# Query and den projection of batches 1 to 3 in one group of sixteen 32x32 TensorE tiles, and a new order of all steps

## The chip, the cores and the metric

The kernel runs on one core of one Trainium2 chip. The metric is the device time of one execution in microseconds, as the median of several runs. A core has five engines with a queue each: PE (TensorE, matrix products into PSUM), DVE (VectorE), ACT (ScalarE), POOL (GpSimd) and SP (SyncE, which here issues most DMAs). Each queue is worked off in order, and an instruction waits until what it reads is written and what it overwrites has been read.

## The reference

Two layers follow each other: a polynomial-sketch attention with 4 batches, 4 heads, 1088 tokens and head size 32 (r = 8), and a feed-forward layer of width 2048 with the activation h * sigmoid(beta * h).

```python
def phi(x):
    a = np.einsum('rd,bhsd->bhsr', S1, x)
    b = np.einsum('rd,bhsd->bhsr', S2, x)
    return np.einsum('bhsi,bhsj->bhsij', a, b).reshape(*x.shape[:-1], r * r)
q_p, k_p = (phi(q), phi(k))
kv = np.einsum('bhsf,bhsd->bhfd', k_p, v)
z = np.sum(k_p, axis=2)
num = np.einsum('bhsf,bhfd->bhsd', q_p, kv)
den = np.einsum('bhsf,bhf->bhs', q_p, z)[..., None] + 1e-06
x = (num / den).transpose(0, 2, 1, 3).reshape(4352, 128)
...
h = x @ w_in
g = h * (1.0 / (1.0 + np.exp(-beta * h)))
return (g @ w_out).astype(np.float32)
```

There is no softmax: kv and z of a batch are sums over all its tokens, so the queries of a batch can only be finished after its keys.

## The kernel before, in words

Attention runs in float32, the feed-forward layer in float16. Tokens of a batch sit on 128 partitions, 34 each; a transpose on DVE turns q and k so that head and feature lie on the partitions (turn_q, turn_k: tokens tq, tk). All work is cut into named steps, and one string, SEQ, is the order in which the steps are written out; each engine gets its instructions in that order, so the string fixes the order of every queue. In the string a token such as `qp2` is the step for batch 2. Where a step can run on two engines, lower case is the first one (POOL for products, ACT for copies) and upper case the second (DVE).

The steps of a later batch b (1 to 3) are these.

- kp, ka (kps, kab): the keys times S1 and S2 on PE, turned on DVE into KAB.
- o (outer): the products of both halves of KAB, 64 features for each key, in four parts, on POOL or DVE.
- va, vb, vc, np, nz: kv on PE (kvz, L586), copied, turned by PE (ndps) and copied into ND.
- g, gm, wz, wm: z is not summed from the 64 features. PE forms the 8x8 products of the two halves over all tokens (gram_g, L599), DVE masks them (gmz), and PE multiplies by S2 (wz_g, L705). This gives W', with which den of a query is the sum over i of (S1 q)_i times (W' q)_i. wm masks W' into a 128x32 matrix with gm.
- qp, qa (qps L488, qab L517): the queries times S1 and S2 in 8 matmuls of 64 rows and 32 columns, turned on DVE into QAB.
- c, ct (c_g L726, c_t L736): the queries times W' in 4 matmuls of 128 rows and 32 columns, turned on DVE.
- cm, cr, cd (L740 to L749): the product with S1 q, the sum, 1e-6 and the reciprocal, and S1 q scaled with it. So the division is done before the features are formed.
- p, t (outer, turn_qo): the 64 features of the queries in four parts, and their transposes on DVE into QT.
- n (num_g, L769): the product with ND in 2 x 16 matmuls of 32x32, into four PSUM banks. x (put_x) copies this into xT, the input of the second layer.

Batch 0 goes another way (aa, ba, ca, ma, da, ia, ra, na, xa and the same with b), and in the first 16 us beta is prepared, w_in is scaled by it (u0 to u3, POOL) and w_out by its inverse (w0 to w7; ACT, or DVE in upper case). `~` is one matmul on constants that keeps PE busy.

The second layer is spread between these steps. A `+` (first, w1) is a "wave": two matmuls of 128x512 into one of two PSUM buffers of two banks, and a Silu on ACT over both (L424, L433). A `-` (second, w2) is two matmuls that add the oldest waiting wave to the output of its chunk of 512 tokens (moeout, L400). There are 68 waves; a `+` does nothing while the tokens of its chunk are not ready. A wave is named here by chunk and number: 6.0 is the first of chunk 6. What is left of both when the string ends follows in a loop (rest).

PSUM has eight banks: four for the two wave buffers (which nps, aps, bps share), two for the buffer "two", one for "one", one for moeout. A buffer is handed on when the last reader of its old content is done, wherever that reader stands in the string.

Of the kernel before, what the change touches and what calls it, by code (L numbers as in the profile page):

```python
# [9 lines left out]
F32 = mybir.dt.float32  # L10
F16 = mybir.dt.float16
ACTF = mybir.ActivationFunctionType
MUL = mybir.AluOpType.mult
# [5 lines left out]
def kernel(  # L19
# [66 lines left out]
    def sb(shape, dtype, name):  # L86
        return const.tile(shape, dtype, tag=name, name=name)
# [125 lines left out]
    nc.vector.memset(hm, 0.0)  # L213
    for h in range(H):
        nc.vector.memset(hm[32 * h : 32 * h + 32, h % 2, :], 1.0)
    gm = sb([P, 4], F32, "gm")
    nc.vector.memset(gm, 0.0)
    for c in range(4):
        nc.vector.memset(gm[32 * c : 32 * c + 32, c : c + 1], 1.0)
    e3 = sb([P, 3], F32, "e3")  # L220
    nc.vector.memset(e3, 0.0)
    nc.vector.memset(e3[:, 1:2], 1.0)
# [34 lines left out]
    sk = sb([P, 2, 2, R], F32, "sk")  # L257
    skc = sk.rearrange("p n m r -> p (n m r)")
    sab = []

    def prep_s(n):
        st_ = sb([P, 4, R], F32, f"st{n}")
        nc.vector.transpose(out=st_.rearrange("p u r -> p (u r)"), in_=sr[n])
        nc.gpsimd.tensor_tensor(out=sk[:, n], in0=st_[:, :2, :], in1=hm, op=MUL)  # L264
        t = sb([P, R, R], F32, f"s{n}")
        nc.scalar.copy(out=t, in_=cut(st_, ([[1, R], [0, R]], [[0, R], [1, R]])[n]))
        sab.append(t.rearrange("p i j -> p (i j)"))

    beta_bc = sb([P, DFF], F32, "beta_bc")

# [227 lines left out]
        kT = kT2[b % 2]  # L498
        project(t, lambda rows, g: kT[rows, NJK * g : NJK * g + NJK, :])

    def qps(b, new=two):
        t = PS["qps", b] = new("qps")
        project(t, lambda rows, g: qT2[b % 2][rows, QB[g] : QB[g] + NJK, :])


    def left_copy(j0, j1, eng):
# [17 lines left out]
        KAB[b] = turn_ab(PS["kps", b], "kab")  # L524

    def qab(b):
        QAB[b] = turn_ab(PS["qps", b], "qab")


    def outer(dst, b, src, nm, j0, j1, eng=None):  # L530
        if b not in dst:
            dst[b] = sbA.tile([P, NJK, H, F], F32, tag=nm, name=nm, bufs=1)
        a0 = src[b][:, 0, j0:j1]
        n = H * (j1 - j0)
        left = cut(a0, [[R, n], [1, R], [0, R]])
        if b == 0 and eng is nc.vector:
            left = cut(KPS[0], [[R, n], [1, R], [0, R]], R * H * j0)
        (eng or nc.vector).tensor_tensor(  # L538
            out=cut(dst[b][:, j0:j1], [[F, n], [R, R], [1, R]]),
            in0=left,  # L540
            in1=cut(a0, [[R, n], [0, R], [1, R]], NJK * H * R),
            op=MUL,
        )

# [156 lines left out]
        )  # L701

    def wz_g(b):
        for g in range(4):
            nc.tensor.matmul(  # L705
                out=PS["gp", b][32 * g : 32 * g + 32, 64 : 64 + H * R],
                lhsT=sr[1],
                rhs=PS["gm", b].rearrange("p h i -> p (h i)"),
                start=True,
                stop=True,  # L710
                skip_group_check=True,
            )

    def wz_m(b):
        t = PS["wz", b] = sbA.tile([P, H, R], F32, tag="wz", name="wz")
        nc.vector.tensor_tensor(
            out=t,
            in0=cut(PS["gp", b], [[R, H], [1, R]], 64),
            in1=cut(gm, [[1, H], [0, R]]),
            op=MUL,  # L720
        )

    def c_g(b, own):
        t = PS["cps", b] = one("cps") if own else PS["kps", b][:, 0]
        for g in range(4):
            nc.tensor.matmul(  # L726
                out=t[32 * g : 32 * g + 32, :JW],
                lhsT=PS["wz", b].rearrange("p h i -> p (h i)"),
                rhs=qT2[b % 2][:, QB[g] : QB[g] + NJK, :],
                start=True,  # L730
                stop=True,
            )

    def c_t(b):
        t = PS["ct", b] = sbA.tile([P, NJK, H, R], F32, tag="ct", name="ct")
        nc.vector.transpose(out=t.rearrange("p j h i -> p (j h i)"), in_=PS["cps", b][:, :JW])  # L736

    def c_a(b, eng):
        t = PS["ct", b]
        eng.tensor_tensor(out=t, in0=t, in1=QAB[b][:, 0], op=MUL)  # L740

    def c_r(b):
        rc = PS["rc", b] = sbA.tile([P, NJK, H], F32, tag="rc", name="rc")
# [3 lines left out]

    def c_d(b, eng):
        eng.tensor_tensor(  # L749
            out=QAB[b][:, 0],  # L750
            in0=QAB[b][:, 0],
            in1=cut(PS["rc", b], [[H, NJK], [1, H], [0, R]]),
            op=MUL,
        )
# [6 lines left out]
        ND[b] = sbA.tile([P, 2, P], F32, tag="nd", name="nd")  # L761
        eng(out=ND[b], in_=t[:, : 2 * P].rearrange("p (c w) -> p c w", c=2))

    def num_g(b, tiles):
        for fc in range(2):
            for h in range(H):
                for g in (2, 0, 3, 1):
                    rows = slice(32 * g, 32 * g + 32)
                    nc.tensor.matmul(  # L769
                        out=tiles[g // 2][32 * h : 32 * h + 32, g % 2, :JW],  # L770
                        lhsT=ND[b][rows, fc, 32 * h : 32 * h + 32],
                        rhs=QT[b][rows, :, h, fc, :],
                        start=(fc == 0),
                        stop=(fc == 1),
                        skip_group_check=True,
                    )

    def put_x(b, i, t, eng):
        x0 = xT[:, b * S + 32 * QB[2 * i] :]
# [86 lines left out]
    def nd_pe(b):  # L866
        PS["ndps", b] = one("ndps")
        nd_g(b, PS["ndps", b])

    def n_g(b):  # L870
        PS["nps", b] = [two("nps"), wave2("nps")]
        num_g(b, PS["nps", b])

    ACT, DVE, POOL = nc.scalar, nc.vector, nc.gpsimd
    DO = {"+": first, "-": second, "~": lambda: keep_warm(1)}
# [24 lines left out]
    for nm, fn in (  # L900
        ("aa", a_A),
        ("ba", b_A),
        ("rb", prep_rbeta),
        ("zt", gram_terms),
        ("zz", gram_z),
        ("da", d_A),
        ("ia", i_A),
        ("kd", kd0),
        ("nd", nd0),
        ("nc", nc0),  # L910
        ("na", n_A),
        ("ab", a_B),
        ("bb", b_B),
        ("db", d_B),
        ("ib", i_B),
        ("nb", n_B),
    ):
        do(nm, fn)
# [20 lines left out]
    for b in range(1, B):  # L939
        for nm, fn in (  # L940
            ("tk", turn_k),
            ("ka", kab),
            ("tq", turn_q),
            ("qa", qab),
            ("gm", gram_m),
            ("wz", wz_g),
            ("wm", wz_m),
            ("ct", c_t),
            ("cr", c_r),
            ("va", kv_a),  # L950
            ("vb", kv_b),
            ("np", nd_pe),
            ("n", n_g),
            ("lv", load_v),
            ("lk", lambda b: load_rows(k, k_t, b, "k")),
            ("lq", lambda b: load_rows(q, q_t, b, "q")),
        ):
            do(f"{nm}{b}", fn, b)
        do2(f"kp{b}", kps, (b,), two, wave2)
        do2(f"g{b}", gram_g, (b,), True, False)  # L960
        do2(f"c{b}", c_g, (b,), True, False)
        do2(f"qp{b}", qps, (b,), two, wave2)
        do2(f"cm{b}", c_a, (b,), POOL, DVE)
        do2(f"cd{b}", c_d, (b,), POOL, DVE)
        do2(f"vc{b}", kv_c, (b,), ACT.copy, DVE.tensor_copy)
        do2(f"nz{b}", lambda b, e: put_ndg(b, PS["ndps", b], e), (b,), ACT.copy, DVE.tensor_copy)
        for n, (j0, j1) in enumerate(JR):
            do2(f"o{b}{n}", lambda b, j0, j1, e: outer(KP, b, KAB, "kp", j0, j1, e), (b, j0, j1), POOL, DVE)
            do2(f"p{b}{n}", lambda b, j0, j1, e: outer(QO, b, QAB, "qo", j0, j1, e), (b, j0, j1), POOL, DVE)
            do(f"t{b}{n}", turn_qo, b, j0, j1)  # L970
        for i in range(2):
            do2(
                f"x{b}{i}",
                lambda b, i, e: put_x(b, i, PS["nps", b][i], e),
                (b, i),
                ACT.copy,
                DVE.tensor_copy,
            )

    SEQ = """  # L980
        ~ s0 ~ bt0 tk00 s1 tk01 kp0 ka0 ~ tqa la ~ ~ lv00 lv01 ~ ~ lv02 bl0 gr ~ lv03 bt1 aa lb zt ba
        ca1 O01 o02 o00 lw1 BL1 zz ~ ca0 be0 bc0 rb v00 o04 v01 lqb ma0 o03 v02 be1 lo0 ma1 lw0 v03 tqb
        bc1 v04 lk1 lw2 da be2 ~ kd bc2 ia nd W0 u0 nc ra0 ~ be3 bc3 ra1 na xa0 xa1 ab u1 CB1 w2 cb0 +
        lq1 ~ u2 w3 lo1 tk1 lv1 bb - u3 mb1 w1 mb0 + kp1 + + ka1 g1 o13 o10 - + - tq1 w4 lv2 gm1 wz1 QP1
        nb O12 wm1 qa1 db w7 o11 + ib + c1 ct1 - lq2 w5 xb cm1 lk2 - + cr1 va1 vb1 CD1 w6 p12 lq3 + - +
        lk3 VC1 - - + np1 + p10 NZ1 - - + p11 p13 - + t12 - - t11 t10 t13 + n1 x10 x11 - + tq2 tk2 kp2 +
        - + lv3 ka2 tk3 g2 o22 + gm2 o20 qp2 wz2 o23 wm2 qa2 + - + c2 + ct2 CM2 - + kp3 + - cr2 + CD2
        p22 p21 p23 O21 - t22 + va2 vb2 vc2 + p20 ka3 + tq3 t23 - - + - t20 np2 + t21 - NZ2 - + n2 x20
        g3 gm3 + X21 wz3 wm3 qp3 + + c3 - + - + qa3 ct3 - O33 o31 + cm3 O32 - cr3 - CD3 + p32 - + O30 -
        + p30 va3 + t32 - P33 + vb3 + - VC3 P31 + - + - np3 + t31 t30 - t33 - + NZ3 n3 - X30 X31 + - - +  # L990
        + - - + - + - - + - + - + - - + - + - + - - + - + - + - - + - + - + - - + - + - + - + - - - -
    """
    for s_ in SEQ.split():
        DO[s_]()
# [30 lines left out]
```

## Time and profile before

| | |
|---|---|
| median of 3 runs | 102.26 us (101.84 to 102.65) |
| profiled execution | 102.28 us, span 100.3 us from first to last instruction |
| granted TensorE clock | 0.996 |
| busy: PE, ACT, DVE, POOL | 93.8, 79.3, 59.7, 34.7 us |
| first wave starts | 16.39 us |
| last n (nps of batch 3) ends | 73.5 us |
| PE ends | 96.77 us |
| Silu on ACT | 68 of 1.02 us, 65.6 us |

In the views, L and a number is a line of the kernel, "out<-in" are the tiles written and read, a bracket at the end is the time in which the engine sat idle before the instruction and what ended it. A float32 matmul shows as two instructions, so "x16" of kps are eight matmuls. Durations of neighbours on one engine overlap slightly.

### The profile page before, as it was taken

Reading aid. Unit: us, or ns where it says so; the run is one execution under the profiler, and the core shown is the slowest. Engines: PE = TensorE matmul, PEld = TensorE weight load, DVE = VectorE, ACT = ScalarE, POOL = GpSimd, SP = SyncE. Lnnn points to the kernel's source line nnn. Section 1 sums busy time; section 2 is a strip of 40 time slices with the busy share of each in tenths; the row PEclk is TensorE's granted clock in tenths of the full one; section 3 lists DMA queues with packets and bytes.
Section 4 is the critical chain, followed back from the end, with each engine's and each line's share of the span. In section 5 each row is a group of like instructions: output and inputs, shape, how many; then the busy total and the mean of one; then the engine's idle time right before and its main releaser. Section 6 shows DMA issues by size and latency. Waiting matters only on the chain.

```text
span 100.3 us, 2886 instructions
## 1 busy us (share of the span) xinstructions
PE 93.8 (93%) x1189; PEld 45.7 (46%) x1189; DVE 59.7 (59%) x129; ACT 79.3 (79%) x103; POOL 34.7 (35%) x41
## 2 busy tenths in 40 slices
PE   5969988999999999999999999999998999999960
PEld 2325732334365443434654434555434444545750
DVE  4759798897876985687894579559463011020220
ACT  1524758997999979899998699999847999999930
POOL 5228686569339601924990032800000000000000
PEclk9999999999999999999999999999999999999998
DMA  2999999999960780023000230006000413202243
GB/s 66 290 213 286 399 405 372 208 205 286 396 241 2 112 218 6 7 41 64 7 0 2 49 60 0 0 0 108 3 0 13 72 20 64 48 9 50 50 78 78
DMA packets 22876, 11.35 MB, mean 113 GB/s; under 512 B 18320, under 2 KB 20688, under 8 KB 22864
## 3 DMA queue, kind: packets, MB, share of 16 engines
q1 hardware_dynamic: 22480, 11.06, 42.3%
q8 instruction: 9, 0.15, 0.7%
q10 hardware_dynamic: 352, 0.11, 0.4%
q0 software_dynamic: 32, 0.02, 0.1%
q14 instruction: 3, 0.02, 0.1%
HBM read 8.95 MB, written 2.23 MB: 111 GB/s over the span
## 4 chain that ended last, share of the span: by engine, by line
PE 85%; DMA 4%; ACT 3%; DVE 2%; issue 2%; POOL 0%; DVEq 0%; POOLq 0%
PE wave L424 31%; PE moeout L400 27%; PE kvz L586 5%; PE nps L769 5%; DMA sr<-in_S_dram 4%; PE kps L488 3%; PE kvz L196 2%; PE qps L488 2%; PE cps L726 2%; PE moeout L368 2%; PE aps L562 1%; PE betaps L286 1%; PE dps L641 1%; ACT g L433 1%; PE ndps L635 1%
## 5 line engine op out<-in xcount | busy, mean ns | idle before, releaser
L433 ACT ACTIVATE g<-wave 128x1024 f16<-128x1024 f32 x68 | 65.6, 1024 | 7.1 <-PE wave L424 6.6
L424 PE MATMUL wave<-xT,winp 128*128 128x512 f16 (+1 forms) x144 | 40.1, 370 | 0.5 <-DVE xT L785 0.3
L400 PE MATMUL moeout<-g,woutp 128*128 128x512 f16 x128 | 35.7, 380 | 0.2 <-ACT g L433 0.2
L424 PEld LDWEIGHTS <-winp 128*128 128x128 f16 x144 | 15.1, 115 | 16.2 <-issue 3.9
L400 PEld LDWEIGHTS <-woutp 128*128 128x128 f16 x128 | 12.1, 98 | 14.9 <-issue 2.5
L410 DVE STREAM_TRANSPOSE o_sb<-moeout 128x512 f32<-128x512 f32 x8 | 5.7, 716 | 20.1 <-PE moeout L400 14.7
L538 POOL TENSOR_TENSOR kp<-kab 128x512 f32<-128x512 f32 (+2 forms) x11 | 12.4, 1157 | 8.7 <-DVE kab L517 6.7
L538 POOL TENSOR_TENSOR qo<-qab 128x512 f32<-128x512 f32 (+1 forms) x10 | 12.0, 1230 | 7.1 <-DVE qab L749 7.1
L549 DVE STREAM_TRANSPOSE qt<-qo 128x512 f32<-128x512 f32 (+1 forms) x12 | 8.7, 756 | 2.1 <-POOL qo L538 1.9
L196 PE MATMUL kvz<-idle 128*128 128x448 f16 x22 | 6.8, 432 | 1.1 <-DVE idle L99 1.1
L306 POOL TENSOR_TENSOR winp<-w_in_sb,beta_bc 128x512 f16<-128x512 f32 x4 | 5.2, 1317 | 2.1 <-DMA w_in_sb<-in_moe_w_in_dram 2.1
L586 PE MATMUL kvz<-kp,v 128*32 128x64 f32 x288 | 5.3, 221 | 0.0
L740 POOL TENSOR_TENSOR ct<-ct,qab 128x288 f32<-128x288 f32 x2 | 2.2, 1110 | 8.8 <-DVE ct L736 8.8
L466 DVE STREAM_TRANSPOSE qT<-q 128x1088 f32<-128x1088 f32 (+2 forms) x5 | 5.2, 1050 | 0.0
L460 DVE STREAM_TRANSPOSE kT<-k 128x1088 f32<-128x1088 f32 (+2 forms) x5 | 5.2, 1049 | 0.0
L586 PEld LDWEIGHTS kvz<-kp,v 128*32 128x32 f32 x288 | 4.3, 110 | 1.8 <-issue 1.2
L517 DVE STREAM_TRANSPOSE kab<-kps 128x288 f32<-128x288 f32 x8 | 3.3, 457 | 2.5 <-PE kps L488 2.5
L769 PE MATMUL nps<-qt,nd 32*32 32x288 f32 x192 | 4.8, 413 | 0.0
L320 ACT ACTIVATE woutp<-w_out_sb,rbeta 128x128 f16<-128x128 f32 x14 | 4.6, 398 | 0.0
L538 DVE TENSOR_TENSOR kp<-kab 128x512 f32<-128x512 f32 (+1 forms) x5 | 4.5, 922 | 0.0
L196 PEld LDWEIGHTS <-idle 128*128 128x128 f16 x22 | 2.4, 117 | 4.0 <-issue 2.2
L488 PE MATMUL kps<-kT,sk 64*32 64x288 f32 x64 | 3.1, 415 | 1.0 <-POOL sk L264 1.0
(100 smaller groups left out, 73.9 us busy)
## 6 DMA issues: line engine op xcount, KB each, us to landing
v<-in_v_dram SPq DMA_DIRECT2D x15, 144.0 KB, 5.3
k<-in_k_dram SPq DMA_DIRECT2D x3, 544.0 KB, 7.1
q<-in_q_dram SPq DMA_DIRECT2D x3, 544.0 KB, 6.4
out_dram<-o_sb SPq DMA_DIRECT2D x20, 64.0 KB, 1.9
w_out_sb<-in_moe_w_out_dram SPq DMA_DIRECT2D x2, 512.0 KB, 8.2
w_in_sb<-in_moe_w_in_dram SPq DMA_DIRECT2D x2, 256.0 KB, 4.7
w_in_sb<-in_moe_w_in_dram SPq DMA_DIRECT2D x1, 512.0 KB, 7.7
k<-in_k_dram SPq DMA_DIRECT2D x1, 288.0 KB, 2.9
```

The costliest lines, as they stand in the source:

```text
L196: nc.tensor.matmul(out=kvz0[:, F:], lhsT=idle, rhs=cut(idle, [[0, 7], [1, F]]), start=fresh, stop=True, skip_group_check=True,)
L306: eng.tensor_tensor(out=winp[:, c], in0=w_in_sb[:, c], in1=beta_bc[:, c], op=MUL)
L400: nc.tensor.matmul(out=moe["acc"][:, :tw], lhsT=woutp[:, j, :], rhs=g[jj], start=(j == 0), stop=(j == NJ - 1),)
L410: nc.vector.transpose(out=o_sb[:, :nt, :].rearrange("p t d -> p (t d)"), in_=moe["acc"][:, :tw])
L424: nc.tensor.matmul(out=wv[:, jj // per, o : o + tw], lhsT=win_unit(j0 + jj), rhs=xT[:, t0 : t0 + tw], start=True, stop=True,)
L433: nc.scalar.activation(out=g[:, :, :gw], in_=wv[:, :, :gw], func=ACTF.Silu)
L460: nc.vector.transpose(out=kT2[b % 2][:, t0:t1].rearrange("p t s -> p (t s)"), in_=k_t[b][:, t0:t1].rearrange("p t d -> p (t d)"),)
L488: nc.tensor.matmul(out=t[32 * g : 32 * g + 32, pi, :JW], lhsT=skc[rows, :], rhs=moving(rows, g), start=True, stop=True,)
L538: (eng or nc.vector).tensor_tensor(out=cut(dst[b][:, j0:j1], [[F, n], [R, R], [1, R]]), in0=left, in1=cut(a0, [[R, n], [0, R], [1, R]], NJ ...
L549: nc.vector.transpose(out=QT[b][:, j0:j1].rearrange("p j h c s -> p (j h c s)"), in_=QO[b][:, j0:j1].rearrange("p j h f -> p (j h f)"),)
L586: nc.tensor.matmul(out=KVZ[b][32 * h : 32 * h + 32, :F], lhsT=v_t[b][:, h, j, :], rhs=KP[b][:, j, h, :], start=(j == 0), stop=(j == NJK - ...
L769: nc.tensor.matmul(out=tiles[g // 2][32 * h : 32 * h + 32, g % 2, :JW], lhsT=ND[b][rows, fc, 32 * h : 32 * h + 32], rhs=QT[b][rows, :, h, ...
```

## The change

For batches 1 to 3 the query projection and the den projection become one. A 32x32 weight matrix sq per parity of the batch holds eight columns of S1, eight of S2 and eight of W', and eight of zeros. It is repeated on the four row groups, one for each head; W' differs from head to head. qps is then 16 matmuls of 32x32: the row group is the head, the column group the quarter of the tokens, and each head has a PSUM bank of its own. They fill "two" and a wave buffer. qab turns both with two transposes of 128x576. c_g, c_t, the mask gm and the masked W' go; wz_g writes eight columns per head, and wm copies them into sq. The constant columns of sq are filled once on POOL (token sq). c_a, c_d and the outer products of the queries read QAB with a step of 32. n is cut into m (first half of the features) and n. SEQ is a new string.

```diff
+    sq = [sb([P, 32], F32, f"sq{n}") for n in range(2)]
...
+    def prep_sq():
+        for t in sq:
+            nc.gpsimd.memset(t[:, 3 * R :], 0.0)
+            for n in range(2):
+                nc.gpsimd.tensor_copy(out=t[:, R * n : R * n + R], in_=st[n][:, 0, :])
...
-    def qps(b, new=two):
-        t = PS["qps", b] = new("qps")
-        project(t, lambda rows, g: qT2[b % 2][rows, QB[g] : QB[g] + NJK, :])
+    def qps(b):
+        PS["qps", b] = [two("qps"), wave2("qps")]
+        for g in range(4):
+            for h in (2, 0, 3, 1):
+                rows = slice(32 * h, 32 * h + 32)
+                nc.tensor.matmul(
+                    out=PS["qps", b][h // 2][32 * g : 32 * g + 32, h % 2, :JW],
+                    lhsT=sq[b % 2][rows, :],
+                    rhs=qT2[b % 2][rows, QB[g] : QB[g] + NJK, :],
...
     def qab(b):
-        QAB[b] = turn_ab(PS["qps", b], "qab")
+        o = QAB[b] = sbA.tile([P, NJK, H, 32], F32, tag="qab", name="qab")
+        for n in (1, 0):
+            nc.vector.transpose(
+                out=cut(o, [[32, 2], [32 * H, NJK], [1, 32]], 64 * n),
+                in_=PS["qps", b][n][:, :, :JW].rearrange("p m (j c) -> p m j c", j=NJK),
+            )
...
     def wz_g(b):
-        for g in range(4):
+        for h in range(H):
             nc.tensor.matmul(
-                out=PS["gp", b][32 * g : 32 * g + 32, 64 : 64 + H * R],
+                out=PS["gp", b][32 * h : 32 * h + 32, 64 : 64 + R],
                 lhsT=sr[1],
-                rhs=PS["gm", b].rearrange("p h i -> p (h i)"),
+                rhs=PS["gm", b][:, h, :],
...
     def wz_m(b):
-        t = PS["wz", b] = sbA.tile([P, H, R], F32, tag="wz", name="wz")
...
+        nc.vector.tensor_copy(out=sq[b % 2][:, 2 * R : 3 * R], in_=PS["gp", b][:, 64 : 64 + R])
...
-    def c_g(b, own):
...
-    def c_t(b):
...
+    def m_g(b):
+        PS["nps", b] = [two("nps"), wave2("nps")]
+        num_g(b, PS["nps", b], 0)
+
     def n_g(b):
-        PS["nps", b] = [two("nps"), wave2("nps")]
-        num_g(b, PS["nps", b])
+        num_g(b, PS["nps", b], 1)
...
+        ~ tk00 lb lv00 ~ s0 s1 lv01 bt0 tk01 ~ kp0 ~ lv02 bl0 ka0 lv03 ~ bt1 tqa ~ ~ ~ gr lqb zt ~ la
+        o02 lw0 aa BL1 ba lk1 ca0 zz be0 bc0 lw2 o00 ~ ~ CA1 v00 o04 ma0 o01 ma1 be1 tqb da ia bc1 v01
+        v02 be2 ra1 o03 bc2 v03 v04 kd u0 tk1 ra0 be3 nd nc ~ lw1 bc3 lo0 ~ na xa0 xa1 ab cb0 u2 lq1 +
+        lo1 u1 CB1 bb rb mb1 w3 + kp1 w0 mb0 + ka1 + g1 W1 nb gm1 u3 wz1 + db w2 o12 - wm1 + tq1 o11
+        w5 ib xb lv1 - lk2 lk3 O10 lq2 - sq o13 W4 - qp1 w7 + qa1 CM1 va1 vb1 w6 cr1 CD1 + - + - - P11
+        p10 - vc1 + + np1 t11 - lq3 NZ1 - + - t10 p13 p12 t13 t12 + - tk2 - + m1 n1 x10 - x11 + kp2 tq2
+        + - + ka2 g2 tk3 + o21 gm2 wz2 wm2 lv2 lv3 - + o22 qp2 qa2 - CM2 o20 cr2 + + CD2 va2 P20 o23 vb2
+        + VC2 - + - t20 + - np2 + p21 p23 - + t21 - t23 + kp3 ka3 NZ2 + p22 t22 - + - + g3 m2 gm3 n2 wz3
+        tq3 - x20 + - wm3 X21 qp3 qa3 + - + o32 - + - CM3 + O30 O33 o31 va3 cr3 + CD3 - + - + P33 - +
+        vb3 + - t33 VC3 + p32 np3 - + P31 p30 t31 t30 t32 NZ3 - + - - + m3 n3 x30 + - X31 - - + + - - +
...
```

The old string, from which the steps above are moved, begins like this and ends each batch in the order named in the prediction.

```
~ s0 ~ bt0 tk00 s1 tk01 kp0 ka0 ~ tqa la ~ ~ lv00 lv01 ~ ~ lv02 bl0 gr ~ lv03 bt1 aa lb zt ba
ca1 O01 o02 o00 lw1 BL1 zz ~ ca0 be0 bc0 rb v00 o04 v01 lqb ma0 o03 v02 be1 lo0 ma1 lw0 v03 tqb
bc1 v04 lk1 lw2 da be2 ~ kd bc2 ia nd W0 u0 nc ra0 ~ be3 bc3 ra1 na xa0 xa1 ab u1 CB1 w2 cb0 +
lq1 ~ u2 w3 lo1 tk1 lv1 bb - u3 mb1 w1 mb0 + kp1 + + ka1 g1 o13 o10 - + - tq1 w4 lv2 gm1 wz1 QP1
nb O12 wm1 qa1 db w7 o11 + ib + c1 ct1 - lq2 w5 xb cm1 lk2 - + cr1 va1 vb1 CD1 w6 p12 lq3 + - +
...
t20 np2 + t21 - NZ2 - + n2 x20
g3 gm3 + X21 wz3 wm3 qp3 + + c3 - + - + qa3 ct3 - O33 o31 + cm3 O32 - cr3 - CD3 + p32 - + O30 -
+ p30 va3 + t32 - P33 + vb3 + - VC3 P31 + - + - np3 + t31 t30 - t33 - + NZ3 n3 - X30 X31 + - - +
...
```

More of the change, by code (lines that the diff above doesn't have):

```diff
@@ L215 @@
         nc.vector.memset(hm[32 * h : 32 * h + 32, h % 2, :], 1.0)
[L216 to L219, printed above, removed]
     e3 = sb([P, 3], F32, "e3")
@@ L259 @@
     sab = []
+    sq = [sb([P, 32], F32, f"sq{n}") for n in range(2)]
+    st = []
     def prep_s(n):
@@ L267, in prep_s @@
         sab.append(t.rearrange("p i j -> p (i j)"))
+        st.append(st_)
+    def prep_sq():
[3 more added lines that the diff above has]
+                nc.gpsimd.tensor_copy(out=t[:, R * n : R * n + R], in_=st[n][:, 0, :])
     beta_bc = sb([P, DFF], F32, "beta_bc")
@@ L499, in kps @@
         project(t, lambda rows, g: kT[rows, NJK * g : NJK * g + NJK, :])
-    def qps(b, new=two):
-        t = PS["qps", b] = new("qps")
-        project(t, lambda rows, g: qT2[b % 2][rows, QB[g] : QB[g] + NJK, :])
+    def qps(b):
[7 more added lines that the diff above has]
+                    rhs=qT2[b % 2][rows, QB[g] : QB[g] + NJK, :],
+                    start=True,
+                    stop=True,
+                )
     def left_copy(j0, j1, eng):
@@ L526, in qab @@
     def qab(b):
-        QAB[b] = turn_ab(PS["qps", b], "qab")
+        o = QAB[b] = sbA.tile([P, NJK, H, 32], F32, tag="qab", name="qab")
[3 more added lines that the diff above has]
+                in_=PS["qps", b][n][:, :, :JW].rearrange("p m (j c) -> p m j c", j=NJK),
+            )
     def outer(dst, b, src, nm, j0, j1, eng=None):
@@ L541, in outer, with outer_q @@
             in1=cut(a0, [[R, n], [0, R], [1, R]], NJK * H * R),
+            op=MUL,
+        )
+    def outer_q(b, j0, j1, eng):
+        if b not in QO:
+            QO[b] = sbA.tile([P, NJK, H, F], F32, tag="qo", name="qo", bufs=1)
+        a0 = QAB[b][:, j0:j1]
+        n = H * (j1 - j0)
+        eng.tensor_tensor(
+            out=cut(QO[b][:, j0:j1], [[F, n], [R, R], [1, R]]),
+            in0=cut(a0, [[32, n], [1, R], [0, R]]),
+            in1=cut(a0, [[32, n], [0, R], [1, R]], R),
             op=MUL,
@@ L714, in wz_m, with c_a @@
     def wz_m(b):
-        t = PS["wz", b] = sbA.tile([P, H, R], F32, tag="wz", name="wz")
[L716 to L720, printed above, removed]
-        )
-    def c_g(b, own):
[L724 to L732, printed above, removed]
-    def c_t(b):
[L735 to L740, printed above, removed]
+        nc.vector.tensor_copy(out=sq[b % 2][:, 2 * R : 3 * R], in_=PS["gp", b][:, 64 : 64 + R])
+    def c_a(b, eng):
+        t = PS["ct", b] = sbA.tile([P, NJK, H, R], F32, tag="ct", name="ct")
+        eng.tensor_tensor(
+            out=t, in0=QAB[b][:, :, :, 2 * R : 3 * R], in1=QAB[b][:, :, :, :R], op=MUL
+        )
     def c_r(b):
@@ L749, in c_d @@
         eng.tensor_tensor(
-            out=QAB[b][:, 0],
-            in0=QAB[b][:, 0],
+            out=QAB[b][:, :, :, :R],
+            in0=QAB[b][:, :, :, :R],
             in1=cut(PS["rc", b], [[H, NJK], [1, H], [0, R]]),
@@ L762, in put_ndg, with num_g @@
         eng(out=ND[b], in_=t[:, : 2 * P].rearrange("p (c w) -> p c w", c=2))
[L764 to L776, printed above, removed]
+    def num_g(b, tiles, fc):
+        for h in range(H):
+            for g in (2, 0, 3, 1):
+                rows = slice(32 * g, 32 * g + 32)
+                nc.tensor.matmul(
+                    out=tiles[g // 2][32 * h : 32 * h + 32, g % 2, :JW],
+                    lhsT=ND[b][rows, fc, 32 * h : 32 * h + 32],
+                    rhs=QT[b][rows, :, h, fc, :],
+                    start=(fc == 0),
+                    stop=(fc == 1),
+                    skip_group_check=True,
+                )
     def put_x(b, i, t, eng):
@@ L903 @@
         ("rb", prep_rbeta),
+        ("sq", prep_sq),
         ("zt", gram_terms),
@@ L943 @@
             ("tq", turn_q),
+            ("qp", qps),
             ("qa", qab),
@@ L947 @@
             ("wm", wz_m),
-            ("ct", c_t),
             ("cr", c_r),
@@ L952 @@
             ("np", nd_pe),
+            ("m", m_g),
             ("n", n_g),
@@ L960 @@
         do2(f"g{b}", gram_g, (b,), True, False)
-        do2(f"c{b}", c_g, (b,), True, False)
-        do2(f"qp{b}", qps, (b,), two, wave2)
         do2(f"cm{b}", c_a, (b,), POOL, DVE)
@@ L968 @@
             do2(f"o{b}{n}", lambda b, j0, j1, e: outer(KP, b, KAB, "kp", j0, j1, e), (b, j0, j1), POOL, DVE)
-            do2(f"p{b}{n}", lambda b, j0, j1, e: outer(QO, b, QAB, "qo", j0, j1, e), (b, j0, j1), POOL, DVE)
+            do2(f"p{b}{n}", lambda b, j0, j1, e: outer_q(b, j0, j1, e), (b, j0, j1), POOL, DVE)
             do(f"t{b}{n}", turn_qo, b, j0, j1)
@@ L980 @@
     SEQ = """
[L981 to L991, printed above, removed]
+        ~ tk00 lb lv00 ~ s0 s1 lv01 bt0 tk01 ~ kp0 ~ lv02 bl0 ka0 lv03 ~ bt1 tqa ~ ~ ~ gr lqb zt ~ la
+        o02 lw0 aa BL1 ba lk1 ca0 zz be0 bc0 lw2 o00 ~ ~ CA1 v00 o04 ma0 o01 ma1 be1 tqb da ia bc1 v01
+        v02 be2 ra1 o03 bc2 v03 v04 kd u0 tk1 ra0 be3 nd nc ~ lw1 bc3 lo0 ~ na xa0 xa1 ab cb0 u2 lq1 +
+        lo1 u1 CB1 bb rb mb1 w3 + kp1 w0 mb0 + ka1 + g1 W1 nb gm1 u3 wz1 + db w2 o12 - wm1 + tq1 o11 +
+        w5 ib xb lv1 - lk2 lk3 O10 lq2 - sq o13 W4 - qp1 w7 + qa1 CM1 va1 vb1 w6 cr1 CD1 + - + - - P11
[4 more added lines that the diff above has]
+        vb3 + - t33 VC3 + p32 np3 - + P31 p30 t31 t30 t32 NZ3 - + - - + m3 n3 x30 + - X31 - - + + - - +
+        - + - + - - + - + - + - + - - + - + - + - + - - + - + - + - + - - + - + - + - + - + - - -
     """
```

## The prediction

> **What bounds the kernel now.** I read the page's busy line first, then the 40 slices, then the chain that ended last, then that chain in order of time, and last the timelines of the places that the change touches.
>
> The page says that PE is busy 93% of the span. The stretches say where: I asked for the busy time of each engine in seven windows, in the columns window, us, PE (count), PEld, DVE, ACT, POOL, granted clock, DMA share, GB/s.
>
> ```profile
> 0.00:16.40 16.40, 13.70 (x233) 6.74 (x234) 11.82 (x43) 7.46 (x19) 9.02 (x20) 1.00 0.92 286
> 16.40:24.40 8.00, 7.76 (x115) 3.01 (x115) 7.21 (x12) 7.79 (x14) 6.00 (x5) 1.00 1.02 243
> 24.40:37.00 12.60, 12.60 (x191) 6.30 (x188) 10.45 (x19) 10.90 (x14) 6.22 (x7) 1.00 0.65 202
> 37.00:55.50 18.50, 18.50 (x286) 8.49 (x289) 12.93 (x25) 17.00 (x19) 9.59 (x8) 1.00 0.12 22
> ...
> 73.50:97.00 23.50, 23.21 (x136) 12.51 (x136) 4.84 (x9) 19.99 (x21) 0.00 (x0) 1.00 0.23 39
> ```
>
> From 24.4 us on PE never pauses, at a granted clock of 1.00. ACT is second (17.0 of 18.5 us), and in 16.4 to 24.4 DVE and ACT are nearly as full as PE. So from the first wave (16.39 us) to PE's end (96.77) the time is PE's work plus its waits, and a saving on PE counts in full unless something else then comes late.
>
> The chain in order of time gives the price of each PE group, as start, length, what.
>
> ```profile
> 40.91 0.65 PE qps L488 x16
> ...
> 42.74 0.43 PE wave L424 x2
> 43.17 0.62 PE cps L726 x8
> 43.79 0.55 PE wave L424 x2
> ...
> 53.93 1.53 PE nps L769 x63
> ```
>
> A wave or a moeout pair costs 0.43 us, and 0.11 more when it follows a small-tile group (0.55). The present query projection is 0.65, the den projection 0.62. The only 32x32 group with 288 columns is nps: 32 matmuls in 64 passes in 1.53 us, 24 ns a pass.
>
> **The change, part by part.**
>
> *PE work.* (1) c_g goes: 3 x 0.62 = -1.86. (2) qps changes from 8 matmuls of 64x32 (16 passes, 0.65) to 16 of 32x32 (32 passes). By the nps row that is 32 x 24 ns = 0.77; bounds 0.65 (it costs what qps costs now) and 0.95 (0.62 of c_g added for half again as much). I take 0.77, the row of the same shape: 3 x 0.12 = +0.36. (3) wz_g keeps four matmuls, 8 columns wide instead of 32: kept at 0.20 (gp L705). (4) n splits into m and n, standing side by side: 2 x 0.77 for 1.53, nothing. (5) I counted, in the two orders, the waves and moeouts that follow a small-tile group: 19 before, 18 after: -0.11. (6) One of the keep-warm matmuls (0.29) stood after the first wave and does not any more: -0.29. The sum of (1) to (6) is -1.90. The same ledger over the old order gives 78.9 us from first wave to end against 80.38 in the trace, so 1.5 us of PE's time there is waits.
>
> The Trainium skill, "TensorE: Matmul & The Clock Gate", part 3 (Measured speedup vs the span model), says that tiles on different row and column groups run together and that each further tile adds about 4 ns. By that the new group would be about 0.65 + 8 x 0.004 = 0.68, and the whole another 0.3 us shorter; the nps row, at 24 ns a pass, speaks for a floor on the issue instead, and I stay with the row.
>
> *DVE.* qab was two transposes of 128x288 (0.46 each) and ct one (0.47). They become two of 128x576. The nearest row is the 128x576 transpose of rb, 0.78, whose successor started after 0.70; so 1.4 for the pair instead of 1.4 for the three: nothing. Bounds 1.3 (the 0.66 pitch of the 128x512 rows) and 2.0, if scattered 32-element rows are written slower. The five memsets of gm (0.06 each) go in a time when DVE waits for S anyway (0.26 us idle before L263): nothing. Moves between engines: O01 to POOL (-0.68 on DVE), one asb and two ct products to DVE (+0.75, +0.9), x30 to ACT (-0.76). They count where a chain passes, below.
>
> *POOL.* prep_sq is six small operations, 0.10 (a memset) to 0.22 (sk L264) each: 0.6 to 1.3 us, between o11 and o13, at about 22.4 to 23.6. The matmuls that need it come at about 25.4, so it is covered by 1.8 us. All five outers of batch 0 are now on POOL: 7.90 + 4 x 1.08 + 0.53 = 12.75 instead of 11.66.
>
> *The start.* v03 now needs the last outer (12.75). On PE, da, v01, v02, be2 fill the time to 13.2, then v03 and v04 end at 13.6. The copy kd stands behind bc2 on ACT (13.27 to 13.86), so it runs at about 13.85 instead of 13.61; nd, two keep-warm matmuls (before: one behind nd) and na follow in order, and na starts at about 15.15 instead of 14.76. Behind na wait xa0 and xa1 and the first wave: 16.79 instead of 16.39, +0.40. Bounds: 0 (ACT and PE instructions overlap at their ends by 0.05 to 0.08 each) and +0.7 (POOL outers at 1.23 instead of 1.08, the rate of L538 qo). tk1 now stands on DVE ahead of ra0: 13.9 to 15.2, ra0 until 15.6, na ends later (15.8), so it costs nothing here; it costs as much as na would come earlier.
>
> *DMAs.* All loads go through SP in order. I count the MB issued up to each load and take from the trace (issue time plus time to landing of each) when that many had landed: 1.92 MB at 10.7 us, 2.43 at 12.0, 2.69 at 12.7, 3.23 at 14.9, 3.74 at 16.3. After the change lw0 stands at 1.92 (10.7; u0 starts when POOL is free, 12.8), lk1 at 2.46 (12.1; tk1 at 13.9), lw2 at 2.98 (13.9; u2 at 14.1), lw1 at 3.23 (14.9; u1 at 15.4), lo0 at 3.74 (16.3; first read by w3 behind the first silu, 18.1). lqb comes earlier. lq1, lo1 and lv1 keep their place by bytes. lk2, lk3, lq2 and lq3 are wanted from 35 us on. lv2 and lv3 now stand behind the store of chunk 0 on SP (about 32), landing 5 us later; va2 is at 44. None of these decides; if lw2 were 1 us late, u1 and with it the wave 0.2 would still have 1.5 us.
>
> *The first waves.* The first moeout now stands after five waves, not one. Waves alone go at ACT's pace (two wave buffers, one silu 0.97 each, w3 and w0 0.7 each between them). Following the PE order with bb, kp1, g1, nb, wz1 and db as filling, PE waits for mb0 before 0.2, for silu 0.1 before 0.3, and for silu 0.2 before 0.4. Up to the first nps of batch 1, ledger 17.70 against time 18.56: 0.86 of waits; before it was 0.60. So +0.26 (bounds 0 to 0.8).
>
> *The query chain of batch 1.* qps used to need only S and tq. Now it needs sq, so kps, ka, g, gm, wz, wm stand ahead of it: qp1 runs at 25.4 instead of 22.8. On DVE, with the pitches of the rows: tq1 21.6, ib 22.8, xb 24.5, O10 25.2, W4 26.0, qa1 26.4, CM1 27.8, cr1 28.2, CD1 29.3 to 29.8 (before: 29.24). The rows of this chain today:
>
> ```profile
> 28.37 0.38 DVE L746 RECIPROCAL rc<-rc 128x36 f32<-128x36 f32 x1
> 28.78 0.46 DVE L749 TENSOR_TENSOR qab<-qab,rc 128x288 f32<-128x288 f32 x1
> ...
> 31.97 2.95 DVE L549 STREAM_TRANSPOSE qt<-qo 128x512 f32<-128x512 f32 x4
> ```
>
> Then P11 on DVE and three outers on POOL (about 3.5; today four in 4.59) to 33.4, the last transpose to 34.9. PE reaches m1 at 35.2. So it is covered, by 0.3 us only. Behind m1 in PE's queue are n1, kp2 and all waves; ACT's x10 waits for n1. In batch 2 the last inputs of m2 (t22, NZ2) come about 0.6 us ahead of it, in batch 3 (NZ3) about 1.1 ahead. The other new wait is wz2 for gm2 behind tk3 on DVE: 0.1. With small waits of waves for ACT in batch 3 I put +0.15 for both batches.
>
> *The end.* Today the wave 6.0 waits for X30 and X31, both on DVE:
>
> ```profile
> 75.60 0.62 PE L424 MATMUL wave<-xT,winp 128*128 128x512 f16 x2 [0.27 <-DVE xT L785]
> ```
>
> The reader sees 0.27 us lost. In the new order x30 is on ACT and eight waves and moeouts stand between n3 and 6.0: -0.3. In return ACT has 0.64 more to do there, and 23 silus left behind n3 (23 x 0.97 + 0.64 = 22.9) against PE's 23.5: nearly even, so I give 0.2 back.
>
> *Sum:* -1.90 + 0.40 + 0.26 + 0.15 - 0.30 + 0.20 = -1.19. The profiled execution took 102.28 with PE's end at 96.77; the 5.5 us around that (last copy, last store, launch) stay. 102.28 - 1.2 = 101.1 us. The median of the runs is 102.26, so the same.
>
> **The rivals.** A, the forecast: 101.1; with the bounds of its terms 100.3 to 102.0.
>
> B, PE's work alone decides: the start costs nothing (bound 0), the first waves neither, and the end gains its 0.3: 102.28 - 1.90 - 0.30 + 0.15 = 100.2. For it: the waits that I add in the start are of the size of the overlaps that I neglect. Against it: na stands in PE's order behind two keep-warm matmuls.
>
> C, slower: the query chain reaches m late. Its place is PE waiting at m1, m2, m3 for the last qt transpose; it decides once the chain has grown by more than its margin (0.3, 0.6, 1.1). Let the qa pair take 2.0 instead of 1.4, O10 and P11 1.0 each instead of 0.8 and 0.7 (the kp product of DVE took 1.04 beside POOL, 0.69 alone), and POOL's outers 1.23 instead of 1.08 for each 512: +0.6 +0.5 +0.5 = 1.6. In batch 2 and 3, whose chains have fewer products on DVE ahead of them, it is some 1.3. The waits are 1.3, 0.7 and 0.2 = 2.2, and the time 101.1 + 2.2 = 103.3. For it: the chain is longer than before, with PSUM read by two 576-wide transposes in a row. Against it: L736 wrote whole blocks and L517 half blocks of 288 columns in the same 0.46 to 0.47, so the pattern of the output seems to cost nothing. The Trainium skill, "TensorEngine Tiling (Array Packing)", Performance Considerations (PSUM Bottleneck), says just that: tiling speeds TensorE up, not the emptying of PSUM, which may become the limit. By that rule C would be the case; the rows of batch 2 and 3 have DVE idle (12.9 of 18.5 us), which speaks against it.
>
> D, the start is later still: POOL at 1.23 an outer, u0 behind it, and PE waiting for w0 and W1 at the first moeouts: +0.7 instead of 0.40 and 0.8 instead of 0.26, so 101.1 + 0.8 = 101.9.
>
> That the change does not do what it says can hardly be: c_g and c_t are not in the new order at all.
>
> **How the numbers follow.** A 0.45, B 0.20, C 0.20, D 0.15. A change of 1% (1.02 us) is about what a measurement of this kernel tells from none. Faster by over 1%, below 101.24: all of B, 0.6 of A, nothing of C and little of D: 0.49. Slower, above 103.28: half of C and a little for chains that I have not seen: 0.14. Within 1%: 0.37. The range leaves out a tenth on each side: 99.9 (B with qp at its lower bound) to 103.3 (C).
>
> **What would show each step.** Right: the new qps group takes 0.75 to 0.8 us and the wave behind it 0.55; no cps group; PE's work from first wave to end is 77.0 us; the first wave starts near 16.8; na at 15.1; qa in transposes of 0.8; n1 ends near 36.9, n2 near 55, n3 near 71.3; no DVE wait ahead of 6.0; PE ends near 95.6. Wrong: idle time of PE or PEld ahead of m1, m2, m3 released by DVE qt or nd (C); the first moeout later than 22.8 or the first silu later than 17.4 (D); POOL waiting for a load of w_in; qps of 0.9 or more; ACT without a gap from 71 us on and PE waiting for it, which would say that the end is ACT's and PE's savings are lost there.

## The result, and the profile after

The changed kernel takes 103.01 us (median of 9 runs, 102.76 to 103.71), the kernel before 101.96 (101.74 to 102.65). The ratio is 1.0103, with a 95% interval of 1.0072 to 1.0135: 1.0% slower, where 101.1 us was forecast; the time lies inside the stated range, on the side that I had thought unlikely. The profiled execution of the new kernel took 103.49 us, half a microsecond over its median, so its times below are compared within stretches rather than end to end.

The stretches of the new kernel come first, in the columns of the same view of before.

```profile
16.40:24.40 8.00, 7.38 (x99) 2.84 (x100) 6.18 (x13) 7.67 (x13) 6.15 (x11) 1.00 1.05 302
24.40:37.00 12.60, 12.00 (x178) 5.82 (x177) 12.01 (x21) 10.68 (x17) 4.54 (x4) 1.00 0.26 49
37.00:55.50 18.50, 18.46 (x322) 8.63 (x300) 14.36 (x27) 16.75 (x19) 10.91 (x10) 1.00 0.46 102
...
73.50:97.00 23.50, 23.37 (x131) 12.36 (x129) 4.03 (x7) 21.67 (x24) 0.00 (x0) 1.00 0.25 38
```

From 24.4 to 37.0 PE was busy throughout before; now it loses 0.6 us, and in the stretch ahead of it 0.4 more than before. In the last stretch ACT is busy for 21.67 us instead of 19.99. The clock is 1.00 as before.

The chain that ended last shows where. In order of time, with start, length and what:

```profile
21.86 0.17 DVE sq L747
22.02 1.22 DVE qT L471
23.24 0.38 DVE dT L687
23.62 0.02 issue
23.64 1.27 DVE rc L690
24.91 0.02 issue
24.94 0.28 DVE rc L691
25.21 0.02 issue
25.24 0.79 DVE rb L697
26.03 0.02 issue
26.05 0.77 DVE xT L717
26.82 0.04 issue
26.86 0.77 PE qps L511 x30
...
43.23 0.78 PE qps L511 x32
```

For five microseconds the chain runs over DVE, and its longest piece is a very small operation: L690 adds 1e-6 to 128x18 numbers and takes 1.27 us. Before, the same instruction (there L658) took 0.18, and POOL had ended 0.18 us earlier (20.90 + 4.02 = 24.92):

```profile
20.90 4.02 POOL L538 TENSOR_TENSOR kp<-kab 128x768 f32<-128x768 f32 x3 [2.00 <-PE wave L424]
25.10 0.18 DVE L658 TENSOR_SCALAR rc<-dT 128x18 f32<-128x18 f32 x1
```

The timeline of the new kernel shows what ran beside it:

```profile
23.36 1.51 POOL L557 TENSOR_TENSOR kp<-kab 128x768 f32<-128x768 f32 x1
23.64 1.26 DVE L690 TENSOR_SCALAR rc<-dT 128x18 f32<-128x18 f32 x1
...
26.86 0.77 PE L511 MATMUL qps<-qT,sq 32*32 32x288 f32 x30 [0.60 <-DVE xT L717]
```

The addition ends 0.03 us after POOL's product o13 ends (24.87). Behind it on DVE stands xb (L717), the last reader of the PSUM buffer "two" that holds nB; qp1 needs that buffer. Two of its 32 passes went to the wave buffer at 25.60, the rest waited until 26.86.

The table sets the time of each stretch, from one start of n (now m) to the next, against the ledger. Work is worked out, as in the prediction: the PE groups of the order, each at the price that the trace shows for its kind. Waits are the rest of the time.

| stretch | before: time, work, waits | after: time, work, waits |
|---|---|---|
| first wave to n1 | 19.09, 18.49, 0.60 | 19.95, 17.70, 2.25 |
| n1 to n2 | 18.45, 18.44, 0.01 | 18.49, 18.24, 0.25 |
| n2 to n3 | 18.04, 17.79, 0.25 | 16.53, 16.02, 0.51 |
| n3 to PE's end | 24.80, 24.17, 0.63 | 26.20, 25.03, 1.17 |

By this ledger the work fell by 1.90, as forecast (the trace shows the prices; the sum is counted, not measured); the waits grew by 2.69, and the first wave came 0.24 later. Together that is +1.03, PE's end moving from 96.77 to 97.80. Two stretches matter: the first (+1.65) and the last (+0.54). The time in which the trace marks PE as idle grew by only 1.00 us between first wave and end (0.52 before, 1.52 after), because a matmul's shown length covers some of its wait: the two passes at 25.60 are shown as 0.67 us long, and the whole group of 32 takes 0.78.

### The profile page after: what moved, and what is told of

The parts are those of the page before. It is cut to its first block, busy times and chain, and to the rows that moved or that the text cites. A ratio compares the mean times of both kernels' runs of the same rounds, so it can differ in the third digit from the quotient of the medians.

```text
span 101.7 us, 2933 instructions
## 1 busy us (share of the span) xinstructions
PE 94.9 (93%) x1214; PEld 46.2 (45%) x1214; DVE 61.1 (60%) x123; ACT 78.6 (77%) x101; POOL 34.5 (34%) x46
## 4 chain that ended last, share of the span: by engine, by line
PE 81%; DVE 7%; ACT 6%; issue 1%; DVEq 0%; ACTq 0%
PE wave L429 28%; PE moeout L405 23%; PE kvz L196 7%; ACT g L438 5%; PE nps L781 5%; PE kvz L618 4%; PE kps L493 3%; PE qps L511 2%; DVE xT L717 2%; PE betaps L291 1%; PE nps L705 1%; DVE rc L690 1%; DVE qT L471 1%; PE aps L594 1%; PE gp L631 1%
## 5 line engine op out<-in xcount | busy, mean ns | idle before, releaser
L557 POOL TENSOR_TENSOR kp<-kab 128x512 f32<-128x512 f32 (+2 forms) x14 | 15.1, 1105 | 10.5 <-DVE kab L531 8.5
L570 POOL TENSOR_TENSOR qo<-qab 128x512 f32<-128x512 f32 (+1 forms) x8 | 10.9, 1391 | 17.1 <-DVE qab L762 17.1
L196 PE MATMUL kvz<-idle 128*128 128x448 f16 x23 | 7.6, 482 | 1.1 <-DVE idle L99 1.1
L543 DVE STREAM_TRANSPOSE qab<-qps 128x576 f32<-128x576 f32 x6 | 4.3, 762 | 1.7 <-PE qps L511 1.7
L325 ACT ACTIVATE woutp<-w_out_sb,rbeta 128x128 f16<-128x128 f32 x12 | 4.0, 393 | 0.0
L803 ACT CAST xT<-nps 128x576 f16<-128x576 f32 x4 | 2.6, 638 | 1.8 <-PE nps L781 1.7
L511 PE MATMUL qps<-qT,sq 32*32 32x288 f32 x96 | 3.0, 413 | 0.7 <-DVE xT L717 0.6
```

Source lines behind the costliest of these rows:

```text
L196: nc.tensor.matmul(out=kvz0[:, F:], lhsT=idle, rhs=cut(idle, [[0, 7], [1, F]]), start=fresh, stop=True, skip_group_check=True,)
L557: (eng or nc.vector).tensor_tensor(out=cut(dst[b][:, j0:j1], [[F, n], [R, R], [1, R]]), in0=left, in1=cut(a0, [[R, n], [0, R], [1, R]], NJ ...
L570: eng.tensor_tensor(out=cut(QO[b][:, j0:j1], [[F, n], [R, R], [1, R]]), in0=cut(a0, [[32, n], [1, R], [0, R]]), in1=cut(a0, [[32, n], [0, ...
```

## The experiments

The theory at the start was **POOL-hold**: the addition stood still because POOL's product was running, and everything from xb to qp1 stood behind it. Its rival was **order**: the chain to qp1 is late in the new string with or without that. A second theory, **overlap**, was on the end. All ratios are against the kernel before, run on the same chip. Two chips were used, so kernels are compared by their ratios.

**Without the addition.**

```diff
+        if tn == 9:
+            nc.vector.reciprocal(out=rv, in_=cut(dT, [[1, nn], [32, tn]]))
+            return rc
         nc.vector.tensor_scalar_add(rv, cut(dT, [[1, nn], [32, tn]]), 1e-6)
         nc.vector.reciprocal(out=rv, in_=rv)
```

> The new kernel, but the second half of batch 0 takes the reciprocal straight from the turned den: the addition of 1e-6 is left out there. Theory POOL-hold (the 128x18 addition on DVE, 1.26 us instead of 0.18, stood still until POOL's product o13 ended, and xb, the buffer two and qp1 stood behind it): qp1 starts 1.1 us earlier without its 0.6 us of PE idle ahead, and the time falls by 0.9 to 1.2, to about 102.0. Theory order (db stands behind five waves and qp1 behind xb, so the chain is late with or without the hold): only the 0.2 us of the addition itself, to 102.8; the reciprocal, reading what POOL would hold, then takes the 1.1 us in its place.

Measured: ratio 0.9987 (0.9961 to 1.0013), 102.12 us: 1.1% below the new kernel, as POOL-hold said. Its timeline:

```profile
23.24 1.51 POOL L557 TENSOR_TENSOR kp<-kab 128x768 f32<-128x768 f32 x1
23.52 0.27 DVE L691 RECIPROCAL rc<-dT 128x18 f32<-128x18 f32 x1
23.82 0.78 DVE L700 STREAM_TRANSPOSE rb<-rc 128x576 f32<-128x576 f32 x1
24.63 0.76 DVE L720 TENSOR_TENSOR xT<-nps,rb 128x576 f16<-128x576 f32 x1
...
25.47 0.77 PE L511 MATMUL qps<-qT,sq 32*32 32x288 f32 x32
```

The reciprocal and the transpose run at full speed beside the same POOL product (0.27 and 0.78, as before); only the addition had been held. qp1 runs in one piece. First wave to n1 is 18.68 us instead of 19.95, and the later stretches are the same to 0.01 us.

**The constant columns early.** One step is moved, so that POOL's product ends earlier; nothing changes on DVE.

```diff
-mb1 w3 + kp1 w0 ... lq2 - sq o13 W4
+mb1 w3 + sq kp1 w0 ... lq2 - o13 W4
```

> The new kernel with step sq (the constant columns, 0.7 us on POOL) moved ahead to where POOL is idle at 19 to 20.6 us, so that POOL's last key product of batch 1 ends 0.65 us earlier, near 24.2. POOL-hold: the addition on DVE ends 0.65 earlier too, near 24.25, and the time falls by 0.6, to 102.4. Order: POOL's end decides nothing; no change, 103.0.

Measured: 1.0042 (1.0012 to 1.0071), 102.45 us. In its trace POOL's three products end at 23.75 and the addition at 23.79:

```profile
20.17 3.58 POOL L557 TENSOR_TENSOR kp<-kab 128x512 f32<-128x512 f32 x3 [1.05 <-PE wave L429]
...
23.11 0.68 DVE L690 TENSOR_SCALAR rc<-dT 128x18 f32<-128x18 f32 x1
```

**A shorter last product on POOL.** Besides the move of sq, the long product (three columns of tokens) goes to DVE and a shorter one to POOL.

```diff
-lk3 O10 lq2 - sq o13 W4
+lk3 o10 lq2 - O13 W4
```

Its expectation was written beside that of the kernel which changes x30 too and which follows below.

> The same without the change to x30: sq early, O13 on DVE, o10 on POOL. POOL-hold: the addition is 0.2 to 0.4 long, the time 101.9 to 102.1. The difference to the kernel with x30 apart is what X31's wait is worth: 0.3 if ACT's pace at the end counts, 0 to 0.1 if not.

Measured: 0.9992 (0.9963 to 1.0020), 102.01 us, with the addition at 0.23 us. POOL ends at 23.60, so the addition, begun at 23.41, is still held for a moment:

```profile
20.47 3.13 POOL L557 TENSOR_TENSOR kp<-kab 128x512 f32<-128x512 f32 x3 [2.37 <-PE wave L429]
...
23.41 0.23 DVE L690 TENSOR_SCALAR rc<-dT 128x18 f32<-128x18 f32 x1
```

The new kernel, the one with sq early and this one are a series: the addition lasts 1.26, 0.68 and 0.23 us, the ratios are 1.0103, 1.0042 and 0.9992, and the stretch from the first wave to n1 takes 19.95, 19.36 and 18.91 us. That is 1.0 us less of the addition for 1.0 us less of the stretch and 1.1 us (0.0111 x 102) less of time. POOL-hold stands, order as the cause of this loss falls.

**The same in the kernel before.** O12 goes from DVE to POOL, so that POOL's products last longer.

```diff
-nb O12 wm1 qa1 db
+nb o12 wm1 qa1 db
```

> The kernel before, with the key product O12 moved from DVE to POOL, so that POOL works until about 26.0 us and the addition of ib (25.1 us, 0.18 us long now) falls into POOL's products. POOL-hold: the addition takes 0.8 to 1.0 us and ends when POOL's product ends, although DVE has one product less to do; xb and its wave come 0.5 to 0.9 later, and the time rises by 0.2 to 0.8 from 102.1. Theory that the long addition was peculiar to the new kernel (its rows, its buffer): it stays at 0.18 and the time falls by up to 0.3.

```profile
21.07 4.60 POOL L538 TENSOR_TENSOR kp<-kab 128x768 f32<-128x768 f32 x4 [1.70 <-PE wave L424]
...
25.27 0.43 DVE L658 TENSOR_SCALAR rc<-dT 128x18 f32<-128x18 f32 x1
```

The addition, 0.18 in the kernel before, takes 0.43 and ends at 25.70, POOL at 25.67. So the hold is not peculiar to the new kernel. It was touched for only 0.25 us, less than expected, because POOL was done sooner than I had worked out; the time did not change (0.9989, 0.9955 to 1.0023).

**The end.** x30 on ACT and X31 on DVE both write tokens 16 and 17 of each row, since the second and third quarter of the tokens overlap there (QB is 0, 9, 16, 25). So X31 waited:

```profile
73.19 0.64 ACT L803 CAST xT<-nps 128x576 f16<-128x576 f32 x1 [0.47 <-PE nps L781]
...
73.86 0.46 DVE L795 CAST xT<-nps 128x288 f16<-128x288 f32 x1 [3.23 <-ACT xT L803]
...
75.83 4.69 ACT L438 ACTIVATE g<-wave 128x1024 f16<-128x1024 f32 x5 [1.02 <-PE wave L429]
```

In these lines of the new kernel ACT, which is busy for 21.67 of the 23.5 us behind 73.5, then sits idle for 1.02 us.

```diff
+        if b == B - 1 and i == 0:
+            eng(out=x0[:, :JW], in_=t[:, 0, :JW])
+            eng(out=x0[:, JW : JW + 224], in_=t[:, 1, :224])
```

> The new kernel; the first half of xT of batch 3 is written by ACT in two copies without the two token columns that the second half writes again, so X31 on DVE need not wait for x30. Theory overlap (X31 waited 0.65 us for x30, and ACT, which paces the last 20 us, stood idle for 1.0): X31 starts within 0.1 us of x30, the waves behind it come 0.15 (PE's work ahead of them) to 0.6 earlier, and the time falls by 0.3 to 0.5. Rival (the end is PE's alone): by 0.15 at most, not to be told from none.

Measured alone: 1.0094 (1.0064 to 1.0123), 102.93 us, against 1.0103 of the new kernel: not to be told from it. Its trace did what was meant (DVE starts at 72.70, ACT at 72.74, ACT's idle time 0.70; n3 to PE's end 25.87 us instead of 26.20).

The same together with the moves for POOL:

> The new kernel, with nothing left out: sq early, O13 on DVE and o10 on POOL instead of o13 and O10 (so POOL is done near 23.4, before the addition of ib at 23.1 has waited long), and x30 written apart from X31. POOL-hold and overlap: as without the addition, 101.9, less 0.3 for X31: 101.6 to 101.9. If the end does not count: 102.0.

Measured: 0.9939 (0.9912 to 0.9966), 101.67 us. It leaves nothing out and beats both kernels: 0.6% faster than before, and 0.5% (0.0053) below the one that differs from it in x30 alone. The two pairs, 0.1% and 0.5%, lie on both sides of the 0.33 us that the trace shows; that it counts is shown by the second pair, whose intervals hardly overlap, its size is not.

```profile
22.81 0.22 DVE L690 TENSOR_SCALAR rc<-dT 128x18 f32<-128x18 f32 x1
...
71.27 0.46 DVE L795 CAST xT<-nps 128x288 f16<-128x288 f32 x1 [2.52 <-PE nps L781]
71.31 0.40 ACT L804 CAST xT<-nps 128x288 f16<-128x288 f32 x1 [0.47 <-PE nps L781]
```

**The new order with the old projections.** In the new string c and ct are put back (the lines for batch 1 are shown, batches 2 and 3 likewise), sq is taken out, m and n are one step.

```diff
-qp1 w7 + qa1 CM1
+qp1 c1 w7 + qa1 ct1 CM1
```

> The new order with the old projections: qps of eight 64x32 matmuls, c in its own matmuls right behind it, ct behind qa, the mask and the old wz; m and n as one step where n stands. It asks what the order is worth alone. PE does 1.9 us more than in the new kernel. If the group gives what PE's ledger says and nothing else: 103.0 + 1.6 = 104.6. If the group also costs waits (qp waits for W', its two transposes): as little as 103.0.

Measured: 1.0152 (1.0103 to 1.0201), 103.91 us, between its two expectations: by itself the new order is 1.5% slower than the old. It is not quite the pure opposite of the new kernel: without sq on POOL its addition is held for less (0.63 us long). The nearest comparison is the kernel with sq early, 0.68 long: 1.0152 - 1.0042 = 1.1%, about 1.1 us that the group is worth in this order. By the two intervals that is 0.5 to 1.7 us, so the 1.6 that PE's ledger gives are not excluded.

**The group in the old order.** c and ct are taken out of the old string, sq is put ahead of ka1, and qp and qa stand where c and ct stood (in batch 1 behind xb, which frees the buffer "two").

```diff
-gm1 wz1 QP1 nb O12 wm1 qa1 db w7 o11 + ib + c1 ct1 - lq2 w5 xb cm1
+gm1 wz1 nb O12 wm1 db w7 o11 + ib xb + - lq2 w5 qp1 qa1 cm1
```

> The group of sixteen tiles in the old order: c and ct are taken out of the old string, sq is put ahead of ka1, and qp and qa of each batch stand where c and ct stood, behind wm. Theory order (the new string costs what the group saves): the group's saving of about 1.6 us on PE shows, less a few tenths for the later qa: 100.6 to 101.6, below the kernel before. Rival group (the 32x32 group, its transposes and its longer chain cost what c saved): 102 to 103, with PE waiting ahead of n1, n2 or n3 for DVE.

Measured: 1.0394 (1.0358 to 1.0431), 106.01 us, slower than everything else and beyond both expectations. Its trace shows the rival there:

```profile
27.04 0.77 PE L511 MATMUL qps<-qT,sq 32*32 32x288 f32 x30 [0.51 <-DVE xT L717]
...
36.60 0.98 DVE L581 STREAM_TRANSPOSE qt<-qo 128x768 f32<-128x768 f32 x1 [0.16 <-POOL qo L570]
...
37.72 1.59 PE L781 MATMUL nps<-qt,nd 32*32 32x288 f32 x64 [0.98 <-DVE qt L581]
```

PE waits for xb ahead of qp1 and for the last qt transpose ahead of m1. These are 1.5 of the 4.2 us that PE is idle there from the first wave to its end. Another 1.3 us are three waits of qps for a silu, since half of the group goes into a wave buffer (in the new kernel's trace no qps waits for ACT), and 0.8 are waves of batches 2 and 3 waiting for their x. So in the old order the longer query chain (W' ahead of qp, two transposes of 576) and the second buffer cost more than the group saves, and the new string costs less than the old one would with this group.

## Why the prediction was wrong

*PE's work*: right. The qps group takes 0.78 us (forecast 0.77), the wave behind it 0.55, cps is gone. The floor of 24 ns a pass held against the Trainium skill's 4 ns for each further tile ("TensorE: Matmul & The Clock Gate", part 3), by which it would have been 0.68 (the prediction's estimate).

*The query chain of batch 1*: this is the step that failed. It said "ib 22.8, xb 24.5" with qp1 at 25.4, and the chain to m1 "covered, by 0.3 us only", with the pitches of rows from a place where POOL stood still: in the old trace POOL ends at 24.92 and the addition begins at 25.10. In the new order POOL works until 24.87 and the addition was due at 23.6. From the start of dT to that of the instruction behind rb took 2.88 us instead of 1.73, and xb began at 26.05. I had worked out the times of POOL (sq until 23.6, o13 behind it) and those of DVE side by side without asking whether they disturb each other, although the prediction itself used a kp product of 1.04 us "beside POOL, 0.69 alone". PE's end was forecast near 95.6 and came at 97.80; of these 2.2 us, 1.39 are waits of the first stretch (2.25, where 0.86 was forecast), and leaving the addition out takes 1.27 of them away (18.68 us instead of 19.95).

The Trainium skill, "SBUF — State Buffer" (Who interferes with whom), states it: GpSimd and a DVE instruction in a mode that uses both of its SBUF ports lock the same pair, and the later one stands still until the other's whole instruction is done; it counts the operation with a scalar among those that can enter such a mode. The runs agree: in all eight kernels in which the two meet, the addition ends 0.03 to 0.04 us after POOL's product. The addition on the first half of batch 0, which reads PSUM, took 0.17 us at 13.14 beside a POOL product that ran from 12.78 to 14.05. The Trainium skill, "VectorE: DVE Perf Modes" (Why PSUM operands drop a tier), states that a PSUM operand rules out the mode with both SBUF ports, and this addition agrees.

*The place of the wait*: rival C priced a late chain at 103.3, near the time that came, but put it ahead of m1 and into the size of the transposes. The qa pair took 1.45, as taken (1.4), and no wait of PE stands ahead of m1, m2 or m3. The wait is at qp1, and its cause another, so it is luck that 103.3 came near and that the time fell into the range. C's own mechanism is what the old order with the new group shows.

*The start* was +0.40 with the first wave at 16.79. It came at 16.63, and in the other traces of the new order between 15.80 and 16.51, against 16.39 to 16.57 in the old: the term was too high, so rival D falls too. What moves the first wave by 0.8 us between traces of the same order was not tried.

*The first waves*: the size was right, the place not. With the addition left out the waits up to n1 are 0.98 us (18.68 - 17.70), where 0.86 was forecast; but the wait for a silu that the trace shows is 0.39 us ahead of 0.1, not ahead of 0.3 and 0.4. *Batches 2 and 3*: 0.50 instead of 0.15; which waits make up the difference was not tried.

*The end* was -0.30 + 0.20. It was +0.54: the step "x30 is on ACT", done at once with X31 on DVE, overlooked that both write the same two tokens. With x30 written apart 0.33 us of it goes; what makes up the rest was not tried. The chain of the new kernel ends in five silus of about 0.8 to 1.05 us, where that of the kernel before ends in PE's work, so ACT sets the last 5 us, as the prediction's last sign of error had it in part (ACT was not without a gap).

With the two places repaired, the order and the group give 101.67: 0.6% below before, half of the 1.2 us that were forecast.

## What to carry to other kernels

When two engines are moved against each other, list for each short DVE operation on the critical chain what POOL runs at that moment: a duration from a trace holds only for the company that it had there. A saving on the bounding engine is worth what its shortest slack allows; a few tenths of cover are no cover for a chain on which one instruction can grow by 1.1 us. When two engines write one tile, look for columns that both write before counting them as parallel.

## What the runs showed of the hardware

An operation on 18 numbers a partition, 0.18 us alone, stood still for 1.1 us behind a POOL product. Reciprocal (0.27) and 32x32 transposes (0.78) of float32 from SBUF were not slowed by a running POOL product; the addition of a constant was. Groups of 32x32 float32 matmuls with 288 columns cost 24 ns a pass (0.78 us for 32 passes, 1.53 for 64). A pair of 128x128 matmuls behind such a group took 0.55 us instead of 0.43.
